# Attention and feed-forward on one core: later gate and result stores, one load per token half, an earlier read-back of the first gates, wider rings in the last stage

## Chip, cores and metric

The kernel runs on 1 core of one Trainium2 chip. The metric is the device time of one execution in microseconds; the time of a kernel is the median over its runs. Five engines work side by side, each through its own instructions in order: TensorE (PE, with its weight loads as PEld), VectorE (DVE), ScalarE (ACT), GpSimd (POOL) and SyncE (SP). In the stages that this document is about, SP issues all transfers between HBM and the on-chip memory (DMAs). An SP instruction that waits for a semaphore holds back every transfer behind it.

## The reference

Eight batches of attention with 12 heads of 448 rows and 64 columns, with the heads mixed before and after the softmax, and a feed-forward layer behind it:

```python
scores = scale * np.matmul(q, k.transpose(0, 1, 3, 2))
scores = np.einsum('bhij,hg->bgij', scores, w_pre)
attn = softmax(scores)                       # with + 1e-09 in the divisor
attn = np.einsum('bhij,hg->bgij', attn, w_post)
x = np.matmul(attn, v)                       # to 3584 tokens x 768
h = x @ w_in                                 # 768 x 2048
g = h - np.tanh(h)                           # the gate
out = g @ w_out                              # 2048 x 768, float32
```

(`softmax` stands here for the reference's three lines with max, exp and sum.)

## The kernel before

**Number format.** Each operand of the feed-forward part is split into a high and a low part (names ending in h and l) of a narrower format, and a product is three matmuls: high by high, high by low, low by high. The split of a tile is one cast on ACT (`high`, L587; `parts`, L457) and one subtraction on DVE that writes the low part in place of the raw tile (`low`, L590; L458).

**Stages.** The attention part fills the first 868 us and leaves the tokens x in HBM (`xs`). The 3584 tokens then go in 7 blocks of 512 (TB). Block 0 runs alone in 16 steps (f = 0 to 15, one 128-wide slice of the hidden layer each; `Block0.step`, L361), and two more steps finish its gates. The other six blocks go in three pairs (s = 0, 1, 2); a pair's 2 x 2 products of halves are done with seven products in place of eight (the scheme of Strassen and Winograd), on sums of the token halves. A pair is a loop of 8 `pair_step`s (L680), each with 7 products of 9 matmuls. Gates are computed behind the products on ACT and DVE, written to HBM (`gos` for block 0, `gss[s]` for the pairs), and read back later, because the second matrix product needs all of them.

**Results.** `Results.run` (L462) is a generator with the second matrix product: block 0's gates by w_out (`plain`, 8 items of 4 units) and then for each pair 28 items of two units (`seventh`: 7 products, 4 items each; 12 matmuls in a unit). Its units are dealt out into the pair loops, a few behind each product (`res.units`, L691), and the rest between and behind the loops. Before an item it asks for loads two items ahead: `more_gr(n + 2)` for gates (tiles gl, 0.5 MB, 3 buffers) and `more_w2(w2 + 2)` for weights (tiles w2, 0.75 MB, 3 buffers), and for the parts of the next item's gates (`parts(n + 1)`).

**Handovers.** Behind the loop of pair s come HELD + AHEAD = 18, 18 and 14 units (L1354), into which the last gates of the pair (`late.v0` to `v5`) and the token jobs of the next pair are dealt. The document calls these stretches the handovers. The last 52 units run alone (L1365): the last stage.

**Token jobs.** `xq_jobs` (L580) makes seven operands of a pair from four raw token halves: b11, b21, t1, t2, t3, t4, b22. `xr` holds a running sum; t4 is the raw b21 half less xr, and the half is loaded a second time as t4l for that (L1306), because `both("b21")` has by then replaced b21l by its low part. The jobs are pulled one at a time: for the first pair at steps 6, 8, 10, 12, 13, 14 and 15 of block 0 and then in the first pair step.

**Order on SP.** Every engine's order is the program's order (`in_order`, L1372). Stores are put off by counting: `after(n, f)` (L396) puts f into a list, `tick()` is called after each unit and after each product of a pair step, and f runs when its count is used up and it is at the head of the list. Before the change the gate stores of a pair step (`ga` in v0, `gb` and `gs` in v5) and the result stores all have n = 2. In block 0 a gate store is kept in `self.store` and sent in the step after. The work tiles ga, gb and gs have one buffer each, so DVE can't write one until its store has read it; `wa`, the weights of the seven products, has 7 tiles and is loaded 6 products ahead.

Of the kernel before, what the change touches and what calls it, by code (L numbers as in the profile page):

```python
# [179 lines left out]
def kernel_body(  # L180
# [175 lines left out]
    class Block0:  # L356

        def __init__(self):
            self.f, self.old, self.store = 0, None, None

        def step(self, between=None):  # L361
# [5 lines left out]
            if self.store:  # L367
                self.store()
                self.store = None
# [11 lines left out]
            if f % 2:  # L381
                if old:
                    old.d2()
                    old.a3()
                    g = work(("ga", "gb")[f // 2 % 2])
                    old.d3(g)
                    old.d4(g)
                    self.store = lambda: nc.sync.dma_start(gos[:, f - 3 : f - 1], g)
                self.old = Gate(self.h) if f < NF else None
            elif old:  # L390
                old.a1()
                old.a2()
                old.d1()
# [11 lines left out]
    class Results:  # L405

        def __init__(self):
# [13 lines left out]
            self.n_c = self.n_bank = 0  # L421
            self.at = self.run()
# [15 lines left out]

        def more_w2(self, upto):
            while self.n_w2 < min(upto + 1, len(self.w2s)):  # L440
                x = self.n_w2 % 3
                p = ff.w2a if x < 2 else ff.w2b
                ff.w2[self.n_w2] = w = p.tile([P, NK, 2, P], F32R, name=f"w2{x}", tag=f"w2{x}")
# [3 lines left out]
        def more_gr(self, upto):  # L447
            while self.n_gr < min(upto + 1, len(self.grs)):
                ff.gr[self.n_gr] = g = ff.gpl.tile([P, 2, TB], F32R, name="gl", tag="gl")
# [12 lines left out]
        def run(self):  # L462
            w2 = 0
            for n, item in enumerate(self.items):
# [4 lines left out]
                self.more_gr(n + 2)  # L469
                self.parts(n + 1)  # L470
                for x in range(2 if plain else 1):
                    self.more_w2(w2 + 2)
# [55 lines left out]
        def store(self, b, t, h, c):  # L528
            to = out[b * TB + t * TT : b * TB + (t + 1) * TT, h * N2 : (h + 1) * N2]
            after(2 if self.n_gr < len(self.grs) else 0, lambda: nc.sync.dma_start(to, c.rearrange("p c n -> p (c n)")))  # L530
# [49 lines left out]
    def xq_jobs():  # L580
# [22 lines left out]
        both("b21")  # L603
        yield
# [8 lines left out]
        sub("t4l", xr)  # L613
        yield
        high("t4", xr)
        low("t4", xr)
        yield
# [23 lines left out]
    class Late:  # L641
# [4 lines left out]
        def v0(self):  # L646
# [4 lines left out]
            after(2, lambda: nc.sync.dma_start(gss[self.s][:, 0:2, self.q], self.ga))  # L651
# [18 lines left out]
        def v5(self):  # L670
            nc.vector.tensor_add(self.gs[:, 2], self.ga[:, 1], self.gs[:, 0])
            nc.vector.tensor_add(self.gb[:, 0], self.gb[:, 1], self.gs[:, 2])
            after(2, self.store)
# [630 lines left out]
    def xq_loads(s):  # L1304
        ba, bb = 2 * s + 1, 2 * s + 2
        for x, b, h in (("b11l", ba, 0), ("b21l", ba, 1), ("t3l", bb, 0), ("b22l", bb, 1), ("t4l", ba, 1)):  # L1306
# [6 lines left out]
    def between0(f):  # L1313
# [7 lines left out]
        if 6 <= f < NF and f % 2 == 0 or f in (13, 15):  # L1321
# [4 lines left out]
    block0.store()  # L1326
# [5 lines left out]
    for s in range(NS):  # L1332
# [13 lines left out]
        if s + 1 < NS:  # L1346
            xq = xq_jobs()
        job = partial(next, xq, None)
# [51 lines left out]
```

## Time and profile before

| | us |
|---|---|
| median of 3 runs | 1793.09 |
| lowest and highest run | 1781.44 and 1793.70 |
| the profiled execution, its own time | 1794.49 |
| span of the profile | 1792.8 |
| granted TensorE clock, mean over the span | 0.976 |

The profile is of one execution, of which the time is 1.7 us over the span. Where the waits of SP come from in the feed-forward part is read in the table of waits of the DMA queue's own engine, from 868 us on; each row names the waiting line, what ended the wait, the total in us, how often, and the longest one:

```profile
SPq L637 <- PE ps_h L318: 201.5, 88, 9.0
SPq L437 <- PE y L545: 111.9, 40, 5.7
SPq L676 <- DVE gb L672: 87.7, 20, 8.7
SPq L651 <- DVE ga L353: 32.8, 13, 5.4
SPq L530 <- DVE c L562: 32.0, 8, 12.5
SPq L308 <- PE ps_h L318: 31.1, 7, 13.4
SPq L388 <- DVE ga L353: 18.5, 3, 7.2
SPq L388 <- DVE gb L353: 14.3, 3, 6.1
```

L637, L437 and L308 wait for TensorE to leave a tile that the load is to fill. L676, L651 and L388 are gate stores that wait for DVE to finish the gate, L530 result stores that wait for the sum in c. While they wait, no load behind them goes out; whether TensorE feels it is another question, which the prediction takes up.

### The profile page before, as it was taken

The numbers are of one execution on the slowest core, as the hardware profiler recorded it, in microseconds if no ns is written. First come the engines' busy times: TensorE is split into PE (matmuls) and PEld (weight loads), VectorE is DVE, ScalarE is ACT, GpSimd is POOL, SyncE is SP. The second block draws the span as 40 slices with busy tenths as digits, with TensorE's granted clock in tenths as the row PEclk, the third lists the DMA queues.
The fourth block names the chain that finished last, engine by engine and source line by source line (L and its number), as shares of the span: only waits on it lengthen the run. The fifth ranks groups of instructions, "written<-read, shape, count | busy, mean of one in ns | idle before, by whom it ended". The sixth has DMA issues, their size and how long they took to land.

```text
span 1792.8 us, 41167 instructions
## 1 busy us (share of the span) xinstructions
PE 1691.1 (94%) x16068; PEld 1401.2 (78%) x16068; DVE 1215.1 (68%) x2119; ACT 1147.2 (64%) x2016; POOL 405.1 (23%) x574
## 2 busy tenths in 40 slices
PE   8999999999999899989986999899998899999998
PEld 6777777777777677767875778788888888888898
DVE  5676767766777577665377889667776867787323
ACT  5777877777787688766475676455655465665232
POOL 1354554554555455443000000000000000000000
PEclk9999999999999999899998999999999999999999
DMA  8769898786978689665686789988889979888887
GB/s 185 222 210 262 246 247 248 239 248 220 257 248 242 203 248 266 217 209 195 199 292 231 241 300 321 328 280 302 306 322 346 345 260 336 311 314 315 308 324 259
DMA packets 339472, 477.44 MB, mean 266 GB/s; under 512 B 105552, under 2 KB 264016, under 8 KB 339280
## 3 DMA queue, kind: packets, MB, share of 16 engines
q1 hardware_dynamic: 338972, 474.38, 81.1%
q8 instruction: 128, 2.10, 0.5%
q14 instruction: 64, 0.52, 0.1%
q10 hardware_dynamic: 308, 0.43, 0.1%
HBM read 277.09 MB, written 120.59 MB: 222 GB/s over the span
## 4 chain that ended last, share of the span: by engine, by line
PE 60%; DMA 11%; ACT 10%; DVE 10%; issue 5%; POOL 2%; SPq 2%; ACTq 0%; DVEq 0%; POOLq 0%
PE ps_o L965 13%; PE ps_m L1007 8%; PE ps_p L926 7%; PE ps_q L882 5%; PE ps_h L315 4%; PE ps_h L316 4%; PE ps_h L318 4%; PE y L543 3%; PE y L545 3%; PE y L544 3%; DMA t<-s 2%; DVE qa L344 2%; DMA gl<-gs 1%; DMA w<-wo 1%; ACT gh L457 1%
## 5 line engine op out<-in xcount | busy, mean ns | idle before, releaser
L965 PEld LDWEIGHTS ps_o<-wr,e 60*112 60x112 f32 (+1 forms) x5760 | 310.0, 177 | 43.5 <-POOL wr L948 18.7
L965 PE MATMUL ps_o<-wr,e 60*112 60x60 f32 (+1 forms) x5760 | 318.6, 261 | 15.9 <-ACT at L975 7.1
L935 DVE TENSOR_REDUCE mx<-ps_p 128x1 f32<-128x448 f32 x360 | 207.8, 619 | 177.4 <-PE ps_p L926 176.9
L937 ACT ACTIVATE e<-ps_p,mx 128x448 f32<-128x448 f32 x360 | 225.7, 634 | 91.2 <-DVE mx L935 89.2
L543 PE MATMUL y<-w,gh 128*128 128x384 f32 x672 | 230.5, 343 | 24.1 <-DMA w<-ts 7.2
L458 DVE TENSOR_TENSOR gl<-gl,gh 128x1024 fp32r<-128x1024 f32 x92 | 112.6, 1224 | 187.7 <-ACT gh L457 186.8
L545 PE MATMUL y<-w,gl 128*128 128x384 f32 x672 | 230.0, 342 | 0.0
L544 PE MATMUL y<-w,gh 128*128 128x384 f32 x672 | 228.6, 340 | 0.0
L975 ACT COPY at<-ps_o 112x960 f32<-112x960 f32 x156 | 153.9, 987 | 84.3 <-PE ps_o L965 83.8
L926 PE MATMUL ps_p<-t,wpre 60*64 60x448 f32 (+1 forms) x1440 | 181.4, 571 | 10.9 <-DMA t<-s 10.2
L1007 PEld LDWEIGHTS ps_m<-at,vr 112*64 112x64 f32 x3072 | 150.8, 139 | 34.6 <-ACT at L982 13.6
L1007 PE MATMUL ps_m<-at,vr 112*64 112x120 f32 (+1 forms) x3072 | 165.7, 265 | 11.1 <-ACT at L982 5.9
L457 ACT CAST gh<-gl 128x1024 fp32r<-128x1024 f32 x92 | 95.9, 1043 | 123.8 <-DMA gl<-gs 75.0
L543 PEld LDWEIGHTS y<-w,gh 128*128 128x128 f32 x672 | 129.0, 192 | 32.9 <-ACT gh L457 15.3
L948 POOL TENSOR_TENSOR wr<-wpost,zs 128x120 f32<-128x120 f32 x180 | 70.6, 392 | 326.5 <-DVE zs L947 227.8
L544 PEld LDWEIGHTS y<-w,gh 128*128 128x128 f32 x672 | 128.9, 192 | 3.4
L545 PEld LDWEIGHTS y<-w,gl 128*128 128x128 f32 x672 | 128.6, 191 | 1.2 <-DVE gl L458 1.0
L882 PEld LDWEIGHTS ps_q<-kk,qh 64*120 64x120 f32 (+1 forms) x768 | 60.1, 177 | 83.7 <-issue 53.2
L882 PE MATMUL ps_q<-kk,qh 64*120 64x448 f32 (+1 forms) x768 | 124.2, 400 | 1.2 <-DVE kk L834 0.5
L887 DVE COPY s<-ps_q 120x448 f32<-120x448 f32 (+1 forms) x192 | 112.5, 615 | 12.5 <-PE ps_q L882 10.9
L331 ACT ACTIVATE u<-h 128x1024 f32<-128x1024 f32 x56 | 59.6, 1065 | 93.9 <-DVE h L724 73.0
L347 ACT ACTIVATE qb<-u,bias 128x1024 f32<-128x1024 f32 x56 | 64.6, 1153 | 66.3 <-DVE qa L344 66.3
(176 smaller groups left out, 3336.4 us busy)
## 6 DMA issues: line engine op xcount, KB each, us to landing
t<-s SPq DMA_DIRECT2D x342, 210.0 KB
gl<-gs SPq DMA_DIRECT2D x84, 512.0 KB
w<-wo SPq DMA_DIRECT2D x52, 768.0 KB
wa<-ss SPq DMA_DIRECT2D x96, 384.0 KB
w<-ts SPq DMA_DIRECT2D x48, 768.0 KB
wa<-wi SPq DMA_DIRECT2D x72, 384.0 KB
gs<-gs SPq DMA_DIRECT2D x24, 768.0 KB
cr<-in_moe_w_in_dram SPq DMA_DIRECT2D x48, 256.0 KB
```

What stands on the lines that cost most here:

```text
L457: nc.scalar.copy(hi, raw(lo))
L458: nc.vector.tensor_sub(lo, raw(lo), raw(hi))
L543: nc.tensor.matmul(y, gh[:, tok], wh, start=first, stop=False, skip_group_check=True)
L544: nc.tensor.matmul(y, gh[:, tok], wl, start=False, stop=False, skip_group_check=True)
L545: nc.tensor.matmul(y, gl[:, tok], wh, start=False, stop=last, skip_group_check=True)
L882: nc.tensor.matmul(ps[:n, :S], qx[a, hp, :], kx[a, hp % 2], start=(x == 0), stop=(x == 2))
L926: nc.tensor.matmul(pss[r][halves[j], :], wpre[k, :], ts[j][k, :], start=True, stop=True)
L935: nc.vector.tensor_reduce(out=mx, in_=ps, axis=AX.X, op=ALU.max, negate=True)
L937: nc.scalar.activation(e, ps, AF.Exp, bias=mx, scale=1.0, accum_out=zs[:, 0, r : r + 1])
L965: nc.tensor.matmul(ps[:CP, j, c * GP : (c + 1) * GP].rearrange("p (h i) -> p h i", i=GI)[:, :, r * GH : (r + 1) * GH], e[k, c * CP : (c + ...
L975: nc.scalar.copy(ats[i0][:, :, :, at : at + 2 * GI].rearrange("p c h (j i) -> p j (c h) i", j=2), ps[:CP, :, : NC * GP].rearrange("p j (x ...
L1007: nc.tensor.matmul(pv[j * D : (j + 1) * D, r, :n], vt[:, j, c, :], ats[i][:, c, 2 * hp + j, :n], start=(c == 0), stop=(c == NC - 1),)
```

## The change

Five edits:

1. Block 0 keeps its gate stores in a list with the step's number and sends them with `send(late)`.
2. The stores of pair gates get n = 4 (ga) and 5 (gb and gs, but still 2 in the last pair step of a loop), result stores n = 5 while gates are still to be loaded.
3. The second load of a token half goes: t4 is made from b21l while that is still raw, and `both("b21")` moves behind t4. t1's two operations come into one job. For the first pair the jobs are pulled at steps 6, 8 and 10 to 15 of block 0.
4. `parts(0)` is called right after step 15 of block 0 instead of by the first unit.
5. From the end of the third pair loop the loads for results go round a larger ring: weights through the seven tiles of the high token parts and the three w2 tiles, gates through six tiles of the low parts and the three gl tiles. Once all gates of the last pair are stored, `far` lets the generator ask for up to four more items ahead.

```diff
     class Block0:
         def __init__(self):
-            self.f, self.old, self.store = 0, None, None
+            self.f, self.old, self.stores = 0, None, []
+
+        def send(self, late):
+            while self.stores and self.stores[0][0] + late < self.f:
+                self.stores.pop(0)[1]()
         def step(self, between=None):
             f, old = self.f, self.old
             self.f += 1
             if f + 2 < NF:
                 load_w0(f + 2)
-            if self.store:
-                self.store()
-                self.store = None
+            self.send(1)
...
-                    self.store = lambda: nc.sync.dma_start(gos[:, f - 3 : f - 1], g)
+                    self.stores.append((f, lambda: nc.sync.dma_start(gos[:, f - 3 : f - 1], g)))
...
+        def deepen(self):
+            self.deep_w2, self.deep_gr = self.n_w2, self.n_gr
         def more_w2(self, upto):
             while self.n_w2 < min(upto + 1, len(self.w2s)):
                 x = self.n_w2 % 3
+                if self.deep_w2 is not None:
+                    x = (self.n_w2 - self.deep_w2) % (len(XQ) + 3) - len(XQ)
+                if x < 0:
+                    w = ff.xqb.tile([P, HK, TB], F32R, name=XQ[x] + "h", tag=XQ[x] + "h")
...
         def more_gr(self, upto):
             while self.n_gr < min(upto + 1, len(self.grs)):
+                x = -1
+                if self.deep_gr is not None:
+                    x = (len(XQ) - 1 - self.n_gr + self.deep_gr) % (len(XQ) + 2) - 3
+                if x < 0:
+                    g = ff.gpl.tile([P, 2, TB], F32R, name="gl", tag="gl")
+                else:
+                    g = ff.xqb.tile([P, HK, TB], F32R, name=XQ[x] + "l", tag=XQ[x] + "l")[:, :2]
...
-                self.more_gr(n + 2)
+                self.far = min(4, self.far + 1) if ff.stored[NS - 1] == NQ else 0
+                self.more_gr(n + 2 + self.far)
...
-                    self.more_w2(w2 + 2)
+                    self.more_w2(w2 + 2 + self.far)
...
-            after(2 if self.n_gr < len(self.grs) else 0, lambda: nc.sync.dma_start(to, c.rearrange("p c n -> p (c n)")))
+            after(5 if self.n_gr < len(self.grs) else 0, lambda: nc.sync.dma_start(to, c.rearrange("p c n -> p (c n)")))
...
         x_tiles("t1l")
         high("t1", xr)
-        both("b21")
-        yield
         low("t1", xr)
...
-        sub("t4l", xr)
+        sub("b21l", xr)
         yield
+        x_tiles("t4l")
         high("t4", xr)
         low("t4", xr)
+        yield
+        both("b21")
         yield
...
-            after(2, lambda: nc.sync.dma_start(gss[self.s][:, 0:2, self.q], self.ga))
+            after(4, lambda: nc.sync.dma_start(gss[self.s][:, 0:2, self.q], self.ga))
...
-            after(2, self.store)
+            after(5 if self.q < NQ - 1 else 2, self.store)
...
-        for x, b, h in (("b11l", ba, 0), ("b21l", ba, 1), ("t3l", bb, 0), ("b22l", bb, 1), ("t4l", ba, 1)):
+        for x, b, h in (("b11l", ba, 0), ("b21l", ba, 1), ("t3l", bb, 0), ("b22l", bb, 1)):
...
-        if 6 <= f < NF and f % 2 == 0 or f in (13, 15):
+        if 6 <= f < NF and f not in (7, 9):
             next(xq, None)
     while block0.f < NF + 2:
         block0.step(between0)
-    block0.store()
+        if block0.f == NF:
+            res.parts(0)
+    block0.send(-2)
     res.more_w2(2)
...
         if s + 1 < NS:
             xq = xq_jobs()
+        else:
+            res.deepen()
```

More of the change, by code (lines that the diff above doesn't have):

```diff
@@ L421, in __init__ @@
             self.n_c = self.n_bank = 0
+            self.deep_w2 = self.deep_gr = None
+            self.far = 0
             self.at = self.run()
@@ L441, in more_w2 @@
                 x = self.n_w2 % 3
-                p = ff.w2a if x < 2 else ff.w2b
-                ff.w2[self.n_w2] = w = p.tile([P, NK, 2, P], F32R, name=f"w2{x}", tag=f"w2{x}")
+                if self.deep_w2 is not None:
+                    x = (self.n_w2 - self.deep_w2) % (len(XQ) + 3) - len(XQ)
+                if x < 0:
+                    w = ff.xqb.tile([P, HK, TB], F32R, name=XQ[x] + "h", tag=XQ[x] + "h")
+                    w = w.rearrange("p c t -> p (c t)").rearrange("p (c t n) -> p c t n", t=2, n=P)
+                else:
+                    w = (ff.w2a if x < 2 else ff.w2b).tile([P, NK, 2, P], F32R, name=f"w2{x}", tag=f"w2{x}")
+                ff.w2[self.n_w2] = w
                 self.w2s[self.n_w2][1](w)
@@ L448, in more_gr @@
             while self.n_gr < min(upto + 1, len(self.grs)):
-                ff.gr[self.n_gr] = g = ff.gpl.tile([P, 2, TB], F32R, name="gl", tag="gl")
+                x = -1
[5 more added lines that the diff above has]
+                    g = ff.xqb.tile([P, HK, TB], F32R, name=XQ[x] + "l", tag=XQ[x] + "l")[:, :2]
+                ff.gr[self.n_gr] = g
                 self.grs[self.n_gr](raw(g))
@@ L1347, in kernel_body @@
             xq = xq_jobs()
+        else:
+            res.deepen()
         job = partial(next, xq, None)
```

## The prediction

> **What bounds the kernel now.** I read the share of each engine first, then busy times by stage, then the table of TensorE's waits, and then the timeline around each long wait. The page has TensorE busy nearly throughout:
>
> ```profile
> PE 1691.1 (94%) x16068; PEld 1401.2 (78%) x16068; DVE 1215.1 (68%) x2119; ACT 1147.2 (64%) x2016; POOL 405.1 (23%) x574
> ```
>
> The change leaves the attention part alone (the first 868 us, up to the first hidden-layer product), so only the later stages count. Cut at block 0, the three pair loops and the stretches between them, the table of windows says where TensorE stands:
>
> ```profile
> core 0: us, PE busy (x) PEld busy (x) DVE busy (x) ACT busy (x) POOL busy (x), PEclk, DMA share, GB/s
> 868.00:968.00 100.00, 81.95 (x414) 65.10 (x412) 65.25 (x54) 60.67 (x66) 2.27 (x3) 0.93 0.73 249
> 1130.00:1205.00 75.00, 67.06 (x342) 59.00 (x341) 44.60 (x35) 37.14 (x48) 0.00 (x0) 0.95 0.86 298
> 1385.00:1460.00 75.00, 68.58 (x332) 64.07 (x333) 54.76 (x49) 36.40 (x39) 0.00 (x0) 0.91 0.90 320
> 1460.00:1640.00 180.00, 180.00 (x893) 161.39 (x891) 139.77 (x136) 111.43 (x129) 0.00 (x0) 1.00 0.85 309
> 1660.00:1793.00 133.00, 120.54 (x672) 117.03 (x670) 41.42 (x45) 35.39 (x43) 0.00 (x0) 0.99 0.84 297
> ```
>
> The reader should see that the third pair loop (1460 to 1640) has nothing to give: TensorE is busy for all 180 us. Idle are 18.1 us in block 0 with its end, 7.9 and 6.4 us in the two handovers between pairs, 12.5 us in the last stage. Those 45 us, and the lower clock that follows a gap, are all that this change can win. In the last stage the waits are for weights (us in total, times, longest; 3.58 of the second row falls at 1676.55, shown below):
>
> ```profile
> PE y L543 <- DMA w<-ts: 7.2, 5, 4.4
> PE y L543 <- DMA w<-wo: 6.9, 5, 3.6
> ```
>
> **The change, part by part.**
>
> *Block 0's stores: nothing moves.* `send(1)` runs after `self.f += 1`, so a store appended in step f is sent when f + 1 < f + 2, which holds in step f + 1: the same step, the same place behind `load_w0`. `send(-2)` at the end sends what is left, as `store()` did. Cost and gain 0, though SP's wait there matters: below, the store of ga at 946.73 holds back the first wa load, for which TensorE waits until 953.17.
>
> *The end of block 0.* Rows of SP, PE, ACT and DVE in turn:
>
> ```profile
> 946.73 0.32 SPq L388 DMA_DIRECT2D go<-ga  x1
> 947.64 1.63 SPq L637 DMA_DIRECT2D wa<-wi  x2
> ...
> 953.17 0.47 PE L315 MATMUL ps_h<-b11h,wa 128*128 128x512 f32 x1 [3.81 <-DMA wa<-wi]
> ...
> 965.46 0.79 PE L514 MATMUL y<-w,gh 128*128 128x512 f32 x1 [6.32 <-ACT gh L457]
> ...
> 972.86 0.63 PE L315 MATMUL ps_h<-t2h,wa 128*128 128x512 f32 x1
> ...
> 975.72 0.39 PE L315 MATMUL ps_h<-t1h,wa 128*128 128x512 f32 x1
> ...
> 962.52 0.57 ACT L697 COPY h<-ps_h 128x512 f32<-128x512 f32 x1
> ...
> 964.36 1.99 ACT L457 CAST gh<-gl 128x1024 fp32r<-128x1024 f32 x2
> ...
> 946.57 1.76 DVE L590 TENSOR_TENSOR t2l<-xr,t2h 128x1536 fp32r<-128x1536 f32 x1
> ...
> 955.67 1.38 DVE L353 COPY_PREDICATED gb<-qb,t 128x1024 f32<-128x1024 int32 x1
> ...
> 968.44 2.35 DVE L458 TENSOR_TENSOR gl<-gl,gh 128x1024 fp32r<-128x1024 f32 x2
> ```
>
> Today gl[0] is read back as soon as the first unit asks for it, which is behind both last gate steps: cast at 964.36, ready at 968.44 + 1.2 = 969.7. With `parts(0)` after step 15 it stands behind that step's last gate operation (955.67 + 1.38 = 957.1). But by then eight token jobs are done instead of seven, one more DVE operation of 1.76 us, and the last one makes DVE wait for its cast; I put that at 2.2 us. So gl[0] is ready at 957.1 + 2.2 + 1.2 = 960.5, about when product 1 ends, and unit 0 starts there instead of 965.46. What is late next: the two last gate steps moved back by 2.2 + 1.2 us or a little more, say 4, and with them the copy of product 0 (962.52, now 966.5), which product 2 needs. Product 2 starts at 966.5 instead of 972.86, product 3 waits for DVE's add, now also behind a 1.76 us subtraction, to about 970.7 instead of 975.72. That is 5 us won; I take off 1 for the slow clock after the new gap: **-4**. Bounds: -9 (the 6.32 gone, and some 3 of the 4.2 us between 965.46 and gl at 969.7) and +2 (one DVE operation more ahead of the store at 946.73, and the waits only change their place).
>
> *Token half loaded once.* b21l stays raw until t4 is made from it, and both its parts come after. Operations on ACT and DVE stay the same in number; 128 x 3 x 512 x 4 B = 0.79 MB less is loaded per pair. In block 0 the removed loads stood behind w(9) on SP, and no wait there names what came after: 0. In the handovers see below. The price: t2 and t4 are now each subtracted, cast and reduced in one job, so DVE waits for one cast (about 1.5 us) twice per handover. DVE is busy 44.6 of 75 us there, which covers most; if the cover is gone it costs 3. I take +1 per handover and put it into their terms.
>
> *Gate and result stores later, at the handovers.* Rows of the first and then of the second handover, and one window of the second:
>
> ```profile
> 1123.04 0.38 SPq L676 DMA_DIRECT2D gs<-gb  x1
> ...
> 1129.48 0.43 SPq L411 DMA_DIRECT2D w<-wo  x1
> ...
> 1137.27 0.77 PE L514 MATMUL y<-w,gh 128*128 128x512 f32 x1 [6.18 <-DMA w<-wo]
> ...
> 1365.47 0.88 SPq L577 DMA_DIRECT2D t3l<-xs  x2
> ...
> 1370.54 0.37 SPq L676 DMA_DIRECT2D gs<-gb  x1
> ...
> 1371.85 3.57 SPq L530 DMA_DIRECT2D out_dram<-c  x4
> ...
> 1379.48 0.41 SPq L427 DMA_DIRECT2D w<-ts  x1
> ...
> 1386.01 0.66 PE L543 MATMUL y<-w,gh 128*128 128x384 f32 x1 [4.45 <-DMA w<-ts]
> ...
> 1395.00:1400.00 5.00, 2.05 (x12) 1.76 (x11) 4.36 (x5) 1.93 (x3) 0.00 (x0) 1.00 1.04 409
> ```
>
> First handover: counting ticks, a pair step of pair 0 has 7 plus one or two, so five ticks after `v5` is the first unit behind the loop. The stores of gb and gs, 1.31 MB, now follow the weight load of 1129.48 instead of preceding it. At the 298 GB/s of that window that is up to 4.4 us of queue; part of it had drained, so 4. Less 1 for the job chain: **-3**. Bounds: -8 (the whole 6.18 and the slow clock behind it) and +2 (the load waits for the token loads ahead of it anyway, and the chain costs its 3).
>
> Second handover: after the t3l loads SP stands until 1370.54 for DVE's gb, then issues 1.31 MB of gates and 0.79 MB of results before the weights of 1379.48. With both behind, the weights go out some 5 us sooner and the 4.45 us wait goes, with about 1.5 us of slow clock. But the 2.1 MB now fall where the window shows the engines full (1.04 at 409 GB/s); 2.1 less t4l's 0.79 is 1.3 MB, 3.2 us at that rate, of which waits further on pay perhaps 2. With the chain's 1: 4.45 + 1.5 - 2 - 1, **-3**. Bounds: -7 and +2.
>
> Inside the pair loops the later stores let SP go on sooner, but TensorE's waits there are not for loads: 0. Their risk is a rival below.
>
> *Last stage.* From the end of the third pair loop loads go round 10 weight and 9 gate tiles instead of 3 and 3. Rows: two gl issues of the steady stretch, TensorE around the first late item and at its end, the store on the chain of waits, and the DMA at its fullest:
>
> ```profile
> 1722.54 0.32 SPq L437 DMA_DIRECT2D gl<-gs  x1
> ...
> 1726.70 0.32 SPq L437 DMA_DIRECT2D gl<-gs  x1
> ...
> 1676.55 0.41 PE L543 MATMUL y<-w,gh 128*128 128x384 f32 x1 [3.58 <-DMA w<-wo]
> ...
> 1789.06 0.34 PE L545 MATMUL y<-w,gl 128*128 128x384 f32 x1
> ...
> 1660.91 8.44 DMA gs<-gb
> ...
> 1760.00:1765.00 5.00, 4.40 (x24) 4.11 (x24) 0.40 (x1) 1.05 (x1) 0.00 (x0) 1.00 1.03 420
> ```
>
> An item takes 4.16 us when nothing waits (1722.54 to 1726.70). Its loads are 1.31 MB, 315 GB/s, below the 420 that a window shows, so a deep ring can run ahead. The item at 1676.55 is k = 6 of the first slot; it and 24 more follow: 25 x 4.16 = 104.0, where the rows give 1789.4 - 1676.55 = 112.9. Of these 8.9 us some 1.5 stay (the slow matmuls after the gap at 1676, see below): 7.4 to win if no load is late, of which I take 6, since SP still issues in order. Of the gap at 1676 itself the larger part stays: its gates exist only when the store of 1660.91 has landed (8.44 us), SP waits for that, and `far` puts another 0.52 MB gate load ahead of its weights (1.3 us at 420 GB/s); against that, the 1.31 MB of the two loads issued just ahead of the store have long landed in a deep ring, 3.1 us at that rate. Together -2, and a gap of some 2 us is left. **-8** in all; bounds -12 (nothing of the gap left either) and -2 (only the shortened gap).
>
> The sum: -4 - 3 - 3 - 8 = -18. The profiled execution took 1794.5 us (span 1792.8), 1.4 over the median of 1793.1; 1794.5 - 18 = 1776.5, or 1775.1 from the median. I say 1776.
>
> *A rule weighed.* Matmuls of this shape run slower after a gap; here after one of 2.19 us in the second pair loop:
>
> ```profile
> 1247.24 0.41 PE L543 MATMUL y<-w,gh 128*128 128x384 f32 x1 [2.19 <-issue]
> ...
> 1248.01 0.52 PE L543 MATMUL y<-w,gh 128*128 128x384 f32 x1
> ```
>
> From 0.34 us (the row at 1789.06) to 0.52, for about 3 us: hence the 1.5 us that I let stand after the gap of 2 us left at 1676. The Trainium skill, "TensorE: Matmul & The Clock Gate" (Part 1: The HAM clock gate), says that the clock falls to half after at least one idle window of about 3.4 us. By that rule a gap of 2 us costs nothing more and the sum would be -19.5, 1774 to 1775; the row has the slow stretch after 2.19 us already, so I keep -18.
>
> **The rivals.**
>
> *Only the last stage gains.* In block 0 and the handovers ACT and DVE work in order, and a wait that goes there returns as a wait for a cast or a gate; the full DMA window speaks for it, DVE's 44.6 of 75 us against. Then 1793 - 8 = 1785.
>
> *All of it goes.* Bounds -9, -6, -6, -11: 1793 - 32 = 1761. The two handovers' first waits are single loads, which speaks for it; the same full window speaks against.
>
> *Slower: the gates' buffers.* gb has one buffer. The tightest place:
>
> ```profile
> 1081.80 0.37 SPq L676 DMA_DIRECT2D gs<-gb  x1
> ...
> 1085.47 0.40 PE L315 MATMUL ps_h<-b11h,wa 128*128 128x512 f32 x1
> ...
> 1094.02 1.23 DVE L350 TENSOR_TENSOR gb<-qa,u 128x1024 f32<-128x1024 f32 x1
> ```
>
> The store moves from 1081.80 to about 1085.5, where the next product 0 starts, and DVE writes gb again at 1094.02: 8.5 us, where the chain's row has 8.44 for a store behind two loads. If stores take x us, DVE waits x - 8.5 in seven steps of pair 0; from x = 11 on that eats the 18 us, at 13.5 the result is 35 - 18 = 17 us slower, 1810. A store behind one wa load of 0.39 MB should take less than 8.44, which speaks against.
>
> *Block 0's stores do move,* if I misread `send`: the first wa load is then free of 946.73, and its 3.81 us go as well: 1772.
>
> **How the numbers follow.** The forecast, 1769 to 1783, has 0.50; only the last stage 0.24; all of it 0.14; block 0's stores 0.03; slower 0.09. The range 1763 to 1790 leaves out the slower case and half of "all of it" with some of the edges, no more than 0.2. A measurement of this kernel can tell about 1% from no change, 18 us, so the border is 1775, just under the forecast: faster takes 0.24 of the forecast's 0.50, 0.13 and 0.03, together 0.40. Slower by over 1% is the far part of its rival, 0.07. Within 1% is the rest, 0.53.
>
> **What would show it.** Right: the first gh cast before the last two gate steps, TensorE's L514 about 5 us after product 1's start at most, no wait of 4 us or more at the two handovers, after k = 6 a steady 4.16 us per item to the end. Wrong: DVE waiting for a store's DMA at L350, stores of go in other steps than before, weights still late in the last 100 us, a new wait for casts of t2 and t4 at the handovers.

## The result, and the profile after

| | before | after |
|---|---|---|
| median of 20 runs each (us) | 1792.53 | 1781.01 |
| lowest and highest run (us) | 1781.44 and 1802.02 | 1770.22 and 1790.16 |
| the profiled execution's span (us) | 1792.8 | 1780.9 |
| ratio of the times, 95% interval | | 0.9928, 0.9910 to 0.9947 |

The kernel is 11.5 us faster, 0.7%; 1776 was predicted, and a gain of 18 us by the working. 1781 lies inside the forecast of 1769 to 1783. The page after, its line of busy times, and the table of windows (a window's start and end, its length, then busy time of each engine) at the places that the prediction read:

```profile
PE 1689.0 (95%) x16068; PEld 1399.0 (79%) x16068; DVE 1215.3 (68%) x2119; ACT 1146.8 (64%) x2016; POOL 403.4 (23%) x574
```

```profile
868.00:968.00 100.00, 84.18 (x447) 67.69 (x448) 65.82 (x56) 62.25 (x71) 2.90 (x4) 0.95 0.68 239
1130.00:1205.00 75.00, 68.08 (x343) 59.59 (x344) 42.60 (x34) 36.27 (x46) 0.00 (x0) 0.94 0.86 298
1385.00:1460.00 75.00, 62.17 (x309) 57.04 (x308) 49.57 (x45) 33.76 (x35) 0.00 (x0) 0.91 0.86 308
1660.00:1780.00 120.00, 116.38 (x670) 115.77 (x669) 40.26 (x41) 35.31 (x43) 0.00 (x0) 1.00 0.82 320
```

In the last stage TensorE is now idle for 3.6 us of 120 (12.5 of 133 before), and 2.6 of them lie behind its last matmul, which ends at 1777.4. At the two handovers it is no better off than before: 6.9 us idle of 75 at the first (7.9 before), 12.8 at the second (6.4 before). Windows at fixed times shift against the work, though, so the rest of this document measures stretches between marks that both traces have: the first product of block 0, and the start of product 0 of a pair step. "Handover 1" goes from the start of pair 0's last step to the start of pair 1's first step, so that last step is in it; "with the loop behind it" goes on to the start of pair 1's last step. "Handover 2" is the same one pair later. "Last stage" goes from the start of pair 2's last step to the end of TensorE's last matmul, and "behind attention" is the span less the time of the first mark. Each number is that of one profiled execution, in us:

| kernel | block 0 with first pair step | handover 1 | the same with the loop behind it | handover 2 | the same with the loop behind it | last stage | behind attention |
|---|---|---|---|---|---|---|---|
| before | 121.4 | 65.4 | 247.4 | 79.3 | 257.2 | 180.8 | 924.1 |
| after | 116.3 | 68.8 | 249.5 | 82.3 | 260.0 | 167.7 | 910.9 |

The attention part, which is the same program in both, took 868.7 and 870.0 us; over all the profiles of this study it took 861.2 to 874.8. That is more than most edits are worth, so these stretches say more about an edit than one execution's time does.

**Block 0** (timeline rows of SP, TensorE, ACT and DVE, after):

```profile
949.42 0.32 SPq L390 DMA_DIRECT2D go<-ga  x1
...
955.95 0.77 PE L315 MATMUL ps_h<-b11h,wa 128*128 128x512 f32 x1 [5.05 <-DMA wa<-wi]
...
961.45 0.39 PE L535 MATMUL y<-w,gh 128*128 128x512 f32 x1
...
967.71 0.50 PE L315 MATMUL ps_h<-t2h,wa 128*128 128x512 f32 x1 [3.75 <-ACT h L719]
...
959.29 1.03 ACT L477 CAST gh<-gl 128x1024 fp32r<-128x1024 f32 x1
...
960.81 1.20 DVE L478 TENSOR_TENSOR gl<-gl,gh 128x1024 fp32r<-128x1024 f32 x1
```

The first unit starts without a wait (before it waited 6.32 us, and 3.03 more for the low part of its gates), product 2 waits 3.75 us for the copy instead. The store of ga still stands in front of the first wa load.

**Handover 1** (SP's rows, then TensorE's long wait):

```profile
1103.56 0.38 SPq L698 DMA_DIRECT2D gs<-gb  x1
1103.98 0.47 SPq L699 DMA_DIRECT2D gs<-gs  x1
...
1116.83 4.63 SPq L598 DMA_DIRECT2D t3l<-xs  x4
...
1126.75 0.43 SPq L413 DMA_DIRECT2D w<-wo  x1
1127.28 0.38 SPq L698 DMA_DIRECT2D gs<-gb  x1
...
1135.14 0.76 PE L535 MATMUL y<-w,gh 128*128 128x512 f32 x1 [7.95 <-DMA w<-wo]
```

The gate stores do follow the weight load now, as intended (1127.28 behind 1126.75). Yet the load goes out 26.6 us after the stretch's start (1126.75 less 1100.15), where it was 25.4 before (1129.48 less 1104.05), and it lands no faster: TensorE starts 8.4 us after its issue, before 7.8.

**Handover 2** (SP, ACT, TensorE):

```profile
1373.98 0.32 SPq L431 DMA_DIRECT2D w<-ts  x1
...
1378.23 0.62 SPq L698 DMA_DIRECT2D gs<-gb  x1
1378.90 0.47 SPq L699 DMA_DIRECT2D gs<-gs  x1
1381.31 2.37 SPq L551 DMA_DIRECT2D out_dram<-c  x4
1383.77 0.47 SPq L441 DMA_DIRECT2D gl<-gs  x1
1384.29 0.54 SPq L431 DMA_DIRECT2D w<-ts  x1
...
1390.54 1.04 ACT L477 CAST gh<-gl 128x1024 fp32r<-128x1024 f32 x1 [7.11 <-DMA gl<-gs]
...
1381.38 0.41 PE L564 MATMUL y<-w,gh 128*128 128x384 f32 x1 [1.60 <-DMA w<-ts]
...
1392.52 0.66 PE L564 MATMUL y<-w,gh 128*128 128x384 f32 x1 [6.71 <-DMA w<-ts]
...
1423.01 0.69 PE L564 MATMUL y<-w,gh 128*128 128x384 f32 x1 [4.45 <-DVE c L583]
```

Half of what the prediction wanted is there: the weights of 1373.98 go out 24.3 us after the stretch's start (1349.64), where it was 28.1 before (1379.48 less 1351.42), and the wait for them falls from 4.45 to 1.60 us. But the stores that were put off now stand in front of the gates and weights of the next item, and TensorE waits 6.71 us for those weights. The wait for the sums in c grew from 2.35 to 4.45; one of 2.95 for ACT (before, 1399.79) fell to 0.85.

**Last stage** (SP at the last gate store, ACT's casts, and the only wait of TensorE of 0.3 us or more behind 1650):

```profile
1659.07 0.37 SPq L698 DMA_DIRECT2D gs<-gb  x1
...
1663.45 0.33 SPq L441 DMA_DIRECT2D gl<-gs  x1
...
1681.47 0.41 PE L564 MATMUL y<-w,gh 128*128 128x384 f32 x1 [1.01 <-ACT gh L477]
...
1685.73 1.05 ACT L477 CAST gh<-t2l 128x1024 fp32r<-128x1024 f32 x1 [4.37 <-PE y L565]
1689.89 1.05 ACT L477 CAST gh<-b21l 128x1024 fp32r<-128x1024 f32 x1 [3.11 <-PE y L565]
```

The casts come every 4.16 us (here and there 4.71 and then 3.61), the time of an item without waits, and so to the end.

### The profile page after: what moved, and what is told of

It is laid out like the page before. It is cut to its first block, busy times and chain, and to the rows that moved or that the text cites. A ratio compares the mean times of both kernels' runs of the same rounds, so it can differ in the third digit from the quotient of the medians.

```text
span 1780.9 us, 41127 instructions
## 1 busy us (share of the span) xinstructions
PE 1689.0 (95%) x16068; PEld 1399.0 (79%) x16068; DVE 1215.3 (68%) x2119; ACT 1146.8 (64%) x2016; POOL 403.4 (23%) x574
## 4 chain that ended last, share of the span: by engine, by line
PE 67%; DMA 9%; ACT 8%; DVE 8%; issue 4%; POOL 2%; SPq 1%; ACTq 0%; DVEq 0%; POOLq 0%
PE ps_o L987 13%; PE ps_m L1029 8%; PE ps_p L948 8%; PE ps_q L904 6%; PE y L564 5%; PE y L566 5%; PE y L565 5%; PE ps_h L315 5%; PE ps_h L316 5%; PE ps_h L318 4%; DMA t<-s 2%; DVE qa L344 1%; ACT u L331 1%; PE ps_m L870 1%; DMA w<-wi 1%
## 5 line engine op out<-in xcount | busy, mean ns | idle before, releaser
L564 PE MATMUL y<-w,gh 128*128 128x384 f32 x496 | 170.0, 343 | 21.2 <-DMA w<-ts 8.3
L478 DVE TENSOR_TENSOR gl<-gl,gh 128x1024 fp32r<-128x1024 f32 x70 | 85.6, 1223 | 126.4 <-ACT gh L477 122.8
L565 PE MATMUL y<-w,gh 128*128 128x384 f32 x496 | 168.1, 339 | 0.0
L566 PE MATMUL y<-w,gl 128*128 128x384 f32 x424 | 144.7, 341 | 0.0
L909 DVE COPY s<-ps_q 120x448 f32<-120x448 f32 (+1 forms) x192 | 112.9, 616 | 13.1 <-PE ps_q L904 11.9
L564 PEld LDWEIGHTS y<-w,gh 128*128 128x128 f32 x496 | 94.7, 191 | 28.6 <-ACT gh L477 9.3
L477 ACT CAST gh<-gl 128x1024 fp32r<-128x1024 f32 x70 | 72.8, 1040 | 58.1 <-PE y L565 25.7
L347 ACT ACTIVATE qb<-u,bias 128x1024 f32<-128x1024 f32 x56 | 64.6, 1154 | 67.4 <-DVE qa L344 67.4
L909 ACT COPY s<-ps_q 120x448 f32<-120x448 f32 (+1 forms) x192 | 95.6, 540 | 7.1 <-PE ps_q L904 6.7
L565 PEld LDWEIGHTS y<-w,gh 128*128 128x128 f32 x496 | 94.7, 191 | 3.4
```

Source lines behind the costliest of these rows:

```text
L564: nc.tensor.matmul(y, gh[:, tok], wh, start=first, stop=False, skip_group_check=True)
L565: nc.tensor.matmul(y, gh[:, tok], wl, start=False, stop=False, skip_group_check=True)
L566: nc.tensor.matmul(y, gl[:, tok], wh, start=False, stop=last, skip_group_check=True)
L909: eng(sts[i][:n, 2 * hp + j, :], ps[:n, :S])
```

## The experiments

So block 0 and the last stage gained, the handovers lost 6.4 us where the prediction had them gain 6. Three theories of that loss:

- **T1**: at a handover TensorE waits for a weight load that stands behind the token loads on SP's queue, with the DMA engines full. Its place behind those decides, and moving stores around it changes nothing.
- **T2**: the later stores did the harm, since they now land in front of other loads that TensorE needs.
- **T3**: the token jobs in their new order hold up ACT and DVE.

The kernels that ran, in stretches as above (us, from one profiled execution each) and in time. The ratio is to the kernel before, run beside it, with its 95% interval:

| kernel | block 0 with first pair step | handover 1 | with its loop | handover 2 | with its loop | last stage | behind attention | median | ratio |
|---|---|---|---|---|---|---|---|---|---|
| e1_rings | 121.0 | 65.7 | 247.7 | 79.3 | 258.1 | 167.6 | 911.6 | 1782.24 | 0.9944 (0.9917 to 0.9970) |
| e2_late | 121.3 | 67.7 | 247.8 | 80.9 | 258.4 | 177.0 | 921.8 | 1792.26 | 1.0002 (0.9976 to 1.0027) |
| e3_tok | 123.7 | 67.4 | 248.1 | 78.5 | 257.8 | 178.4 | 925.4 | 1797.82 | 1.0032 (1.0005 to 1.0059) |
| e4_p0 | 114.0 | 65.9 | 247.9 | 79.0 | 257.4 | 175.9 | 912.4 | 1786.25 | 0.9962 (0.9932 to 0.9993) |
| e5_two | 113.3 | 66.7 | 248.7 | 80.1 | 257.6 | 168.2 | 904.9 | 1777.89 | 0.9925 (0.9898 to 0.9952) |
| e6_send3 | 111.4 | 65.2 | 247.2 | 78.6 | 257.5 | 167.2 | 900.7 | 1771.40 | 0.9888 (0.9862 to 0.9914) |
| e7_spread | 114.8 | 65.0 | 244.3 | 78.9 | 256.4 | 168.5 | 901.3 | 1770.50 | 0.9890 (0.9851 to 0.9929) |
| e8_soon | 114.8 | 68.0 | 248.8 | 79.0 | 256.7 | 168.2 | 905.9 | 1778.72 | 0.9924 (0.9900 to 0.9948) |
| e9_old | 107.9 | 59.1 | 240.4 | 78.0 | 256.6 | 167.7 | 889.8 | 1763.51 | 0.9837 (0.9790 to 0.9884) |
| e10_soon | 110.6 | 60.2 | 241.0 | 78.7 | 256.2 | 168.7 | 893.8 | 1763.09 | 0.9849 (0.9808 to 0.9890) |
| e11_late | 109.7 | 63.6 | 242.8 | 77.8 | 255.3 | 168.1 | 893.3 | 1765.59 | 0.9858 (0.9814 to 0.9901) |
| e12_shift | 110.7 | 59.7 | 238.3 | 78.5 | 255.9 | 167.6 | 890.0 | 1759.79 | 0.9831 (0.9793 to 0.9870) |

How far a stretch of the same program differs between executions can be read in it. Before, e1, e4, e5 and e6 share the code of both handovers: with the loop behind, 247.2 to 248.7 and 257.2 to 258.1. There, differences below 1.5 us are no finding. Block 0 scatters by 0.5 us among before, e1 and e2, but by 3.6 between e6 and e9, which share its code.

### One edit alone, four times

Each is the kernel before with one edit of the change's diff. e1: `deepen`, the larger rings and `far`. e2: the stores' counts:

```diff
-            after(2 if self.n_gr < len(self.grs) else 0, lambda: nc.sync.dma_start(to, c.rearrange("p c n -> p (c n)")))
+            after(5 if self.n_gr < len(self.grs) else 0, lambda: nc.sync.dma_start(to, c.rearrange("p c n -> p (c n)")))
...
-            after(2, lambda: nc.sync.dma_start(gss[self.s][:, 0:2, self.q], self.ga))
+            after(4, lambda: nc.sync.dma_start(gss[self.s][:, 0:2, self.q], self.ga))
...
-            after(2, self.store)
+            after(5 if self.q < NQ - 1 else 2, self.store)
```

e3: the token half loaded once, with the order of the jobs and their calls in block 0. e4: `parts(0)` behind step 15. Of e1, e3 and e4 these are the lines at the core:

```diff
-                self.more_gr(n + 2)
+                self.far = min(4, self.far + 1) if ff.stored[NS - 1] == NQ else 0
+                self.more_gr(n + 2 + self.far)
...
-        sub("t4l", xr)
+        sub("b21l", xr)
...
-        if 6 <= f < NF and f % 2 == 0 or f in (13, 15):
+        if 6 <= f < NF and f not in (7, 9):
...
+        if block0.f == NF:
+            res.parts(0)
```

> The kernel before with the deep rings of the last stage alone (10 weight and 9 gate tiles, loads up to four more items ahead); stores, token loads, jobs and block 0 as before. All theories expect the last stage to gain what it gained in the whole change, 13.0 us (180.8 to some 167.8 us from the end of the third pair loop), since none of them puts that gain down to another edit, and every stretch ahead of it to stay within 1 us. Time 1780 us, ratio 0.993. If the later stores took part in the last stage, it gains only 8 to 10 us here and the time is 1783 to 1785.

Measured: last stage 167.6, everything ahead of it as before. The rings make the whole gain of that stage. But the three other kernels, which have the small rings, took 177.0, 178.4 and 175.9 us there, where the execution of before took 180.8. The gain is 10.4 us against the mean of those four (178.0), and 13 only against one long execution.

> The kernel before with the gate and result stores begun later, and nothing else. T1 (the handovers are bound by the stream of transfers: the weight load queues behind the token loads, wherever the stores stand): both handovers within 1.5 us of before, 65.4 and 79.3 us, time 1791 to 1794. T2 (the later stores land in front of the gate and weight loads that TensorE needs next, and that is what the change lost): the handovers are 2 to 4 us longer each, some 68 and 82 us, time 1797 to 1799. The prediction's own step had them 4 us shorter each, 1785. Block 0 and the last stage within 1 us in all three.

Measured: 1.0002; handover 1 is 2.3 us longer, but its loop gives 1.9 back; handover 2 is 1.5 longer. With their loops they are 0.4 and 1.2 us longer, inside the scatter. T2's 2 to 4 us are not there, and the gain of 4 us each that the prediction's step had is not either: the later stores are worth nothing by themselves. At handover 2 this kernel's trace has the same pair of waits as the whole change, 1.34 and 6.31 us (1380.10 and 1390.81).

> The kernel before with the token half loaded once, the new order of the jobs and of their calls in block 0, and nothing else. T3 (the jobs that subtract, cast and reduce in one, with the copies and additions of result sums queued behind them, cost the handovers): each handover 2 to 4 us longer than the 65.4 and 79.3 of before, time 1796 to 1800 with block 0 unchanged. T1: 0.79 MB less in the stream of each handover make them 1 to 3 us shorter or leave them, time 1788 to 1793. T2: within 1 us of before. Block 0 by all: within 1.5 us of 121.4.

Measured: 0.3% slower (1.0032). With their loops the handovers are 0.7 and 0.6 us longer, no finding: less to load and the new order of the jobs together bring nothing there and cost nothing, against T3. Whether each is nothing or one pays for the other, this run can't tell. The cost is in block 0, 2.2 us, which no theory had. TensorE's row there in this kernel:

```profile
967.08 0.79 PE L514 MATMUL y<-w,gh 128*128 128x512 f32 x1 [10.43 <-ACT gh L457]
```

The extra jobs in block 0's last steps stand ahead of the first gates' cast. Unit 0 waits for its gates in one piece of 10.43 us; before, it was 6.32 and then 3.03, together 9.35. The wait for the first wa load is longer too, 4.67 us for 3.81.

> The kernel before with the first gates split after block 0's step 15 instead of behind its last two gate steps, and nothing else. All theories put block 0's gain down to this edit: block 0 with the first pair step 116 to 117 us (before 121.4, the whole change 116.3). T1: the first handover then starts 5 us earlier for TensorE, but its weight load is issued hardly sooner, so that the first handover is 2 to 4 us longer than 65.4 and the time is 1788 to 1791. T2 and T3: the handover stays at 65.4 and the time is 1787 to 1788.

Measured: block 0 is 7.4 us shorter, more than in the whole change, where edit 3 takes 2.2 of it. Handover 1 stays at 65.9. T1's expectation that the handover takes 2 to 4 us of it back falls: what TensorE gains ahead of a handover, the loads gain too.

### Two edits, and block 0's stores really later

e5 has e1's and e4's edits. e6 adds the first edit of the change with a count that moves the stores:

```diff
-            self.send(1)
+            self.send(3)
```

> Two of the four edits alone: the deep rings of the last stage and the first gates split after block 0's step 15; stores and token loads as before. If the stretches of the runs with one edit add up, block 0 with the first pair step takes 114 us, the handovers 65.7 and 79.2, the last stage 167.6, and the time is 20 us below before, 1773 (ratio 0.989): 8 us below the whole change. T1, T2 and T3 all expect that, as no run so far shows a gain at a handover. If it isn't below the whole change's 1781, the edits don't add up and the readings by stretches fall.

> The same two edits, with the gate stores of block 0 really later: a store made in step f goes out in step f + 3 and so behind the first loads of wa. If the 5 us wait for the first wa load in front of pair 0's product 0 comes from SP standing at such a store, that wait falls to under 1 us and block 0 with the first pair step is 3 to 5 us shorter, some 110 us. Against it: the gates' tile is written again in step f + 4, so that DVE may wait for the store's landing and give 2 to 4 us back; then the stretch stays at 112 to 115 us.

Measured: e5's median is 1777.9, a miss by 5 us, and by its ratio (0.9925) it can't be told from the whole change (0.9928). By the stretches the edits do nearly add up: behind attention e5 is 19.2 us shorter than before, where e4 had won 7.4 in block 0 and e1 13.2 in the last stage, and 6.0 shorter than the whole change. Its attention part took 873.6 us in the profile, 4.9 more than before. e6: SP's rows and the first matmul of pair 0:

```profile
941.88 4.05 SPq L658 DMA_DIRECT2D wa<-wi  x2
...
948.62 0.50 SPq L390 DMA_DIRECT2D go<-ga  x1
...
946.37 0.47 PE L315 MATMUL ps_h<-b11h,wa 128*128 128x512 f32 x1 [0.34 <-DMA wa<-wi]
```

With the store behind the wa loads, the wait for the first of them falls from 3.85 us in e5 to 0.34, and waits for the first gates' parts (2.49 and 0.99 us), which are made no sooner, take about as much back. Block 0 still gains 1.9 us against e5, below the 3 to 5 expected, and 5.4 in e9, which has the same code there and the same waits for the gates (2.52 and 0.99). What differs are the waits for the weights of block 0's own products, whose loads stood behind such stores as well: 5.3 us in all in e5, 1.9 in e6, none of 0.3 us or more in e9. DVE's wait for a store's landing, the risk named, is 0.42 us in e6. Over all kernels, the means of block 0 with the first pair step are 109.7 us (e6, e9) against 113.6 (e4, e5), and 110.3 (e10 to e12) against 115.3 (after, e7, e8): storing three steps later is worth 4 to 5 us. The change's own first edit could not have done this, since `send(1)` moves nothing.

### The token loads, and the stores, in the whole change

e7 is the whole change with the loads of t3l and b22l in the first units of the handover and not in the last pair step; e8 is the whole change with the three counts of e2's diff back at 2.

```diff
-                    for _ in range((2, 2, 2, 0, 1, 3, 2)[i]):
+                    for _ in range((2, 2, 2, 0, 0, 0, 0)[i]):
```

> The whole change, with the token loads t3l and b22l moved out of the last pair step and into the first units of the handover (numbers 2, 2, 2, 0, 0, 0, 0 in place of 2, 2, 2, 0, 1, 3, 2). T1: the weights that TensorE waits 7.95 us for at the first handover are held by their place behind these loads; now they go out 5 to 10 us earlier, that wait falls to under 3 us, and each handover is 3 to 6 us shorter than the whole change's 68.8 and 82.3. If the amount in the stream binds and not the order, the wait comes back later in the handover as waits for other weights, and the handovers stay within 2 us of 68.8 and 82.3. T2 expects no more than 2 us either, since the late stores stay where they are.

Measured: handovers 3.7 and 3.4 us shorter than after the whole change, as T1 expected, 1770.5 us. SP and TensorE at the first handover of e7:

```profile
1108.90 0.42 SPq L413 DMA_DIRECT2D w<-wo  x1
...
1111.00 4.73 SPq L598 DMA_DIRECT2D t3l<-xs  x4
...
1118.64 0.47 PE L535 MATMUL y<-w,gh 128*128 128x512 f32 x1 [1.75 <-DMA w<-wo]
```

The weights stand ahead of t3l now and go out 19.0 us after the stretch's start (1108.90 less 1089.86), 7.6 us earlier than after the whole change. The wait of 7.95 us has become 1.75, and one of 1.86 for the next weights. The medians show this less surely than the stretches: the interval of e7's ratio overlaps that of the whole change.

> The whole change with the gate and result stores begun as early as before. T2: the handovers go back to 65.4 and 79.3 us, 6 us less in both together, time 1775. T1 with T3: the stores' place is worth no more than 2 us in both together; the handovers stay between 66 and 69, and 80 and 82 us, time 1779 to 1781. Last stage within 1 us of 167.7.

Measured: handover 1 moves by 0.7 us only (T1), handover 2 by 3.3 (T2): each theory is right at one place. At handover 2 of e8, SP and TensorE:

```profile
1374.07 0.32 SPq L431 DMA_DIRECT2D w<-ts  x1
...
1377.53 0.65 SPq L441 DMA_DIRECT2D gl<-gs  x1
1378.22 0.46 SPq L431 DMA_DIRECT2D w<-ts  x1
...
1380.48 0.66 PE L564 MATMUL y<-w,gh 128*128 128x384 f32 x1 [4.48 <-DMA w<-ts]
```

The weights that TensorE waits 4.48 us for are those of 1374.07, as late as before (28.2 us after the stretch's start at 1345.92). The next item's gates go out 31.6 us after that start, without the stores in front, and the weights behind them are not waited for; after the whole change it was 34.1 (1383.77 less 1349.64). So the two waits of 1.60 and 6.71 us are one of 4.48 again. In the medians e8 (0.9924) can't be told from the whole change (0.9928).

### All together

e9 is e6 with e7's diff, so without the edits 2 and 3; e10 is e7 with `send(3)` and e8's counts; e11 is e10 with the late stores; e12 is e10 with the jobs one earlier:

```diff
-            [late.v0], [late.v1, late.v2], [late.v3], [late.v4], [late.v5, job], [job, job], [job, job], [job, job],
+            [late.v0], [late.v1, late.v2], [late.v3], [late.v4], [late.v5, job, job], [job, job], [job, job], [job, job],
```

> Rings, first gates early, block 0's stores three steps later, and the token loads t3l, b22l (and t4l, still loaded twice) moved out of the last pair step; gate and result stores and jobs as before. If the place of the weights behind the token loads is what bound the handovers of the kernel before too (T1), both handovers fall below 65.4 and 79.3: to 61 to 63 and 75 to 77 us, time 1764 to 1767. If the whole change's handovers gained in e7 only because its late stores had done harm there (T2), they stay at 65 and 79 and the time is 1771, that of e6.

Measured: 59.1 us for handover 1, 6.2 less than e6, from which only the place of the token loads differs, and 6.3 less than before: the place behind the token loads bound the kernel before as well. TensorE has no wait of 0.8 us or more for weights there any more. Handover 2 is 0.6 us shorter than in e6 and with its loop 0.9, no finding: what e7 gained there, the late stores had first lost. T1 holds at the first handover. At the second the harm is T2's, but it needs the token loads in the same place, since either remedy, e7's or e8's, took it away. What made handover 1 longer after the change than before (3.4 us, 2.1 with its loop) stays open: with its loop the later stores alone (e2) give 0.4 of it and the new jobs alone (e3) 0.7, both inside the scatter, and with the stores early again (e8) 1.4 is left. The windows of 40 us at the first handover show the DMA engines' busy share and their GB/s in the last two columns. First before:

```profile
1104.00:1144.00 40.00, 33.82 (x163) 28.67 (x162) 30.56 (x28) 21.66 (x24) 0.00 (x0) 0.91 1.00 353
```

After the change:

```profile
1104.00:1144.00 40.00, 32.05 (x157) 27.30 (x156) 26.80 (x25) 18.87 (x20) 0.00 (x0) 0.87 0.97 335
```

In e9, which comes to the handover 7.5 us earlier:

```profile
1104.00:1144.00 40.00, 39.00 (x212) 33.52 (x212) 32.42 (x29) 21.63 (x21) 0.00 (x0) 1.00 1.01 374
```

The engines are as full in e9 as before, and TensorE is busy for 39.0 us of 40 in place of 33.8 (39.0 as well in the 40 us from e9's own start of the stretch): what was wrong was the order of the loads, not their amount. The Trainium skill, "DMA: Bandwidth & Descriptors" (Queues, rings and completion order), says that each DMA engine consumes its descriptors in ring order; the rows agree, as the weights behind the token loads are late (TensorE starts 7.8 us after their issue before, 8.4 after the change) wherever the stores behind them go.

> As the run above, with the token half loaded once and the new order of jobs (so the whole change less its late stores, plus block 0's later stores and the moved token loads). Sum of stretches: block 0 112 to 113, handovers 64 and 77, time 1765 to 1769. T3: 1 to 3 us slower than the run above, by the jobs. T1: equal or 1 to 2 us faster, since 0.79 MB less is in each handover.

> As the run above, with the gate and result stores late again: the whole change plus block 0's later stores and the moved token loads. With the token loads out of the way, T1 expects the late stores to bring what the prediction asked of them, up to 1 to 2 us less per handover than the run above; T2 expects 1 to 3 us more, as in e8 against the whole change. Time 1766 to 1769.

Measured: e10 against e9, block 0 is 2.7 us longer, with the sign of e3 but within the scatter there, and the rest differs by less than 1.5; 0.79 MB less per handover, with the new jobs, brought nothing again. e11 against e10: handover 1 with its loop 1.8 us longer, handover 2 with its loop 0.9 shorter. The medians (1763.1 and 1765.6) can't be told apart. Where the weights have a free way, late stores stand in front of the next ones and cost a little; nowhere do they gain what the prediction asked of them.

> As e10, with one more token job in the first slot that has jobs, so that each subtraction stands at the end of one slot and its cast and the second subtraction in the next. T3: the wait of 4.45 us for the sums' additions in the second handover falls below 2.5, and each handover is 1 to 3 us shorter than in e10. T1 and T2: within 1 us of e10.

Measured: handover 1 with its loop 2.7 us shorter (0.5 of it in the handover itself), handover 2 as in e10. TensorE's wait for DVE's sums at the second handover, in e12:

```profile
1398.64 0.69 PE L564 MATMUL y<-w,gh 128*128 128x384 f32 x1 [3.46 <-DVE c L583]
```

And in e10:

```profile
1403.23 0.69 PE L564 MATMUL y<-w,gh 128*128 128x384 f32 x1 [4.46 <-DVE c L583]
```

The wait for the sums fell by 1.0 us only, against T3's 2; the gain is behind the other handover, where it was not looked for, and what made it is open. The intervals of e10 and e12 overlap. e12 has the lowest median of all, 1759.8 (ratio 0.9831, interval 0.9793 to 0.9870), below both the kernel before and the whole change.

## Why the prediction was right, and where it was wrong

**Block 0's stores, 0:** right, they did not move. The rival, that they move, took the wait of 3.81 us for the first wa load as the gain. Moving them with `send(3)` is worth 4 to 5 us in the means above, so the size was near, but not by that wait alone: the waits for the first gates' parts take it back, and the weights of block 0's own products come sooner.

**The end of block 0, -4:** -5.2 measured. The mechanism was as told: unit 0 without a wait, product 2 late next, waiting for its copy, and that at 966.5 as predicted, less the 1.26 us by which this execution's first product came later. The size is that of two edits against each other: -7.4 for the early `parts(0)` (e4) and +2.2 for the extra jobs (e3). The prediction priced those jobs at 2.2 us of DVE's time, and 2.2 us is what block 0 lost by them. That both agree to 0.1 is in part luck, since e7 and e8, with the same code there, took 1.5 us less than the whole change.

**The handovers, -3 and -3:** wrong; +3.4 and +3.0 were measured, and +2.1 and +2.8 with the loops behind them, outside the bounds of +2 too, and with waits of 4 us or more left at both. The step that failed at the first is "The stores of gb and gs, 1.31 MB, now follow the weight load of 1129.48 instead of preceding it. At the 298 GB/s of that window that is up to 4.4 us of queue". Two things are wrong in it. First, only what left the front of the load was counted. Every pair step has such stores, and all but those of a loop's last step are put off by the same count, so those of the step before come in at the other end. Before, they went out ahead of the last pair step (SP, before):

```profile
1101.10 0.37 SPq L676 DMA_DIRECT2D gs<-gb  x1
1101.52 0.46 SPq L677 DMA_DIRECT2D gs<-gs  x1
```

That is 2.9 us ahead of the stretch's start at 1104.0; after the change the rows at 1103.56 and 1103.98 stand 3.4 and 3.8 us behind its start at 1100.15. So from that start on as many bytes precede the weights as before; this is read from the rows, and e2 agrees, in which the later stores alone shorten nothing. Second, bytes over a rate was the wrong price: the load's place behind the token loads t3l and b22l decides (e7, e9). The prediction had that only in its bound, "the load waits for the token loads ahead of it anyway". The 0.79 MB less of t4l could not help this load: before, t4l goes out at 1129.96, behind it. The second handover's step was right in that the first weights go out sooner, by 3.7 us where some 5 were taken. It had the risk in it, "the 2.1 MB now fall where the window shows the engines full", and priced it at 2 us. It was more than the whole gain: the stores came in front of the gates and weights of the next item, and with the stores early again the handover is 3.3 us shorter (e8).

**The job chain, +1 per handover:** not seen above the scatter in e3, nor in e10 against e9, each together with the loads saved. The cost that is seen was in block 0.

**Inside the pair loops, 0:** right; pair 0's loop, from the start of its second step to that of its last, took 113.8 to 113.9 us in all kernels; pair 1's loop gave 1.3 us back after the change. The rival of the gates' buffers did not come.

**The last stage, -8:** the mechanism was right (e1), the size too small: -13.0 against this execution, outside the bound of -12, and -10.3 against the mean of four without the rings. From the item k = 6 on, 7.4 us went (112.9 before; 105.4 after, from 1671.97 to the end: 25 items of 4.16, a gap of 1.01 and a rest of 0.4), just the 7.4 of the working, of which 6 was taken, as no load was late. The term that was mis-sized is the one ahead of that item: "a gap of some 2 us" was to be left and -2 to be won, and 5.6 us went, with the gap of 3.58 gone from that item altogether and one of 0.96 at 1655.40 gone too. 1.0 us came two items later (1681.47), with no slow matmuls behind it.

The 45 us of idle time, "all that this change can win", were counted too high by the 3.6 us behind the last matmul, which ends at 1789.4 of 1793. The rival "all of it goes" adds less (-6, -6, -11) than the bounds of its parts (-8, -7, -12), with which it would be 1757. Neither bears on the forecast.

The sum, -18 predicted and -11.9 in the span (-5.2 + 3.4 - 1.3 + 3.0 - 0.2 - 13.0, with +1.3 of the attention part and 0.1 at the end): two errors of opposite sign, 12 us too good at the handovers and 5 too little in the last stage. That the time lies inside the forecast is luck to that extent: block 0 and the last stage came for the reasons told, the handovers did not.

**The clock:** the rule weighed made no difference to the outcome, since the gap of 1.0 us left no slow matmuls. What was measured about it stands below.

## What to carry to other kernels

When every store of a loop is put off by the same count, ask what comes into the place before a critical load, and not only what leaves it. Where a load is late on a full queue, move it ahead of loads that are needed later, before making the queue's bytes fewer (here 0.79 MB fewer, with a new order of the jobs, showed no gain): the three numbers changed in e7's diff took 6 us from handover 1 (e9 against e6), where the later gate and result stores took nothing. Measure an edit between marks inside the trace when a stage that it doesn't touch scatters by more than the edit is worth.

## What the runs showed of the hardware

SP took longer to issue the same kind of transfer where the DMA engines were busier: four token loads took 1.74 us together at the start of pair 0's last step in e7 (1091.42), at a DMA share of 0.41 and 104 GB/s, and 4.73 us at 1111.00, at 1.02 and 413 GB/s, in the same execution.

Slow matmuls come after gaps of different lengths, and not always at once. After 2.35 us (before, 1421.92) the first matmul took 0.69 us and those behind it 0.52, in place of 0.33, with a granted clock of 0.50 there. After 3.58 us (before, 1676.55) the first six took 0.33 to 0.44 and the slow ones came 1.3 us later. One and the same gap in pair 1's loop, 2.2 us long, was followed by ten matmuls of 0.52 or more before (1247.24) and after the change (1245.46), and by none in e7 (1231.42). The Trainium skill, "TensorE: Matmul & The Clock Gate" (Part 1: The HAM clock gate), describes a free-running window of about 3.4 us. That fits the delay that differs from gap to gap and the gap that counts in one run and not in another; its one idle window as the condition does not fit slow matmuls after 2.35 us. No run here tells what the condition is.
